# Attention and two mixtures of experts in one program: ScalarE, not SyncE, asks for the expert weights and for the stores of their split halves, one step later each

## The chip, the cores and the metric

The kernel runs on one core of a Trainium2 chip. The metric is device time in microseconds (us) of one execution; lower is better. A profile of one execution stands beside the timed runs.

## What is computed

Inputs are float32 (the two weights of the first feed-forward block arrive as 64-bit numbers and are converted on the chip). Three blocks follow each other:

```python
# 1: attention with 32 memory slots per head (8 batches, 8 heads, 576 positions, 64 wide)
a = softmax(phi); k_m = a^T k; v_m = a^T v
attn = softmax(q k_m^T / 8) v_m          # -> x: 4608 tokens x 512
# 2: a feed-forward block ("first MoE" in the kernel's names), 512 -> 2048 -> 512
x = relu(x @ w_in)**2 @ w_out
# 3: a mixture of 8 experts, one per token, 512 -> 1024 -> 512
e = argmax(x @ w_gate); out = gate * (relu(x @ w1[e]) @ w2[e])
```

Sums have to come out in about float32 accuracy, so a factor x is held as two float16 numbers, hi = f16(s x) and lo = f16(s x - hi), and each product is three matmuls.

## The kernel before

**Stages.** Until about 100 us the weights of block 2 are loaded and converted and the first batch goes through attention. From then to about 850 us the main loop (L1144) runs over 192 iterations n: 12 blocks of 384 tokens by 16 slices of the 2048 hidden columns. An iteration does `g1` (L656: six matmuls of U by attnT into the PSUM tile h, then three ScalarE operations L676, L678, L679 that make r = relu(h), g = r squared as float16 and r squared in float32, then one VectorE operation L680 that makes the low half of g) and, three iterations late, `g2` (L693: nine matmuls L688 of g by wo into acc). There are two buffers of h and four of g. From about 850 us the experts' tiles follow (`tiles`, L1225).

**What runs beside the main loop.** The seven other batches of attention are generators that are moved on in the loop (L1164 to L1181). A routing generator per token block (`route`, L729) makes record tiles rec, has them transposed by DMA (L760, xTb<-rec, asked for by SP), and scatters rows to DRAM (tile scr). `weight_stream` (L592) prepares the experts' weights: 16 matrices (w1 and w2 of eight experts), each in four quarters of 512 KB. Its four stage buffers are wst[c] (in the profile: wstage). For matrix n it takes a maximum of every quarter (w1: VectorE, L185 called from L618) or its sum of squares (w2: ScalarE, L616), works out a scale, and then for each quarter c: ScalarE writes the hi half into a buffer o (two of them; L643), VectorE the lo half (L644), SP stores o to DRAM (L645: ws1 or ws2 <- o) and SP asks for the same quarter of matrix n+1 (L597 or L599, called from L650). The buffers o are named wo in the profile (wo16 in the order of instructions).

**What sets the order.** Every engine works off its own list in order, and a DMA is asked for by an instruction in the list of SP, ScalarE or GpSimd. A scheduler with a simulated timeline puts each engine's list together when the program is built. The loop moves the weight stream on by WSTEPS / (16 * 10 - 4) steps per iteration (L1187); a step ends at a `yield`, of which a matrix has seven. Each DMA signals its landing on one of eight semaphores (DMAHW0 to DMAHW7) taken in turn, and an instruction that asks for a DMA first waits until the earlier DMA on its semaphore has landed.

Of the kernel before, what the change touches and what calls it, by code (L numbers as in the profile page):

```python
# [23 lines left out]
P = 128  # L24
B, H, S, D, M = 8, 8, 576, 64, 32
DM, DFF, NT, E, F = 512, 2048, 4608, 8, 1024
# [11 lines left out]
R0 = 3.0  # L38
R1 = 1.0
R2 = 2.5  # L40
WSTEPS = 2 * E * 7
HP0 = 50
HP1 = 50
UB = 3
# [9 lines left out]
def e23(x):  # L54
    return float(x * (1 << 23))
# [3 lines left out]
def tile_attention__then__moe__then__moe2(  # L59
# [14 lines left out]
    V, A, G, T, SP = nc.vector, nc.scalar, nc.gpsimd, nc.tensor, nc.sync  # L74
# [102 lines left out]
    def pow2_of_squares(t, s, total):  # L177

        ti, si = t.bitcast(I32), s.bitcast(I32)
        V.tensor_scalar(ti, total.bitcast(I32), 24, None, ALU.logical_shift_right)  # L180
        V.tensor_scalar(si, ti, e23(-1), e23(204), ALU.mult, ALU.add)
        V.tensor_scalar(ti, ti, e23(1), e23(59), ALU.mult, ALU.add)

    def absmax(dst, src):
        V.tensor_reduce(dst, src, axis=AX.X, op=ALU.max, apply_absolute_value=True)  # L185
# [406 lines left out]
    def weight_stream():  # L592
        def load(n, c):
            e, which = divmod(n, 2)
            t = wst[c]
            if which == 0:
                SP.dma_start(t, w1[e, c * P:(c + 1) * P, :])  # L597
            else:
                SP.dma_start(  # L599
                    t.rearrange("p (a n) -> p a n", a=2),  # L600
                    w2[e, 2 * c * P:(2 * c + 2) * P, :].rearrange("(a p) n -> p a n", p=P),
                )

        wstage = pw[0].tile([P, 4, 2 * DM], F32, tag="ws", name="wstage", bufs=1)
        wst = [wstage[:, c] for c in range(4)]
        for c in range(4):
            load(0, c)
        yield
        for n in range(2 * E):
            e, which = divmod(n, 2)  # L610
            m = pw[0].tile([P, 6], F32, tag="wm", name=f"wm{n}", bufs=2)
            sums = which == 1
            for c in range(4):
                if sums:
                    jk = wo[:, NF].rearrange("p a d -> p (a d)").bitcast(BF16)
                    A.activation(jk, wst[c], AF.Square, accum_out=m[:, c:c + 1])  # L616
                else:
                    absmax(m[:, c:c + 1], wst[c])  # L618
                if c % 2 == 1:
                    yield  # L620
            V.tensor_reduce(m[:, 4:5], m[:, 0:4], axis=AX.X, op=ALU.add if sums else ALU.max)
            G.partition_all_reduce(m[:, 5:6], m[:, 4:5], P, RED.max)
            yield
            top = 1 if which == 0 else 9
            t = pw[0].tile([P, 1], F32, tag="wt", name=f"wt{n}", bufs=2)
            s = pw[0].tile([P, 1], F32, tag="wsc", name=f"wsc{n}", bufs=2)
            ti, si = t.bitcast(I32), s.bitcast(I32)
            if sums:
                pow2_of_squares(t, s, m[:, 5:6])
            else:  # L630
                V.tensor_scalar(ti, m[:, 5:6].bitcast(I32), 0x7F800000, None, ALU.bitwise_and)
                V.tensor_scalar(ti, ti, e23(40), None, ALU.max)
                V.tensor_scalar(si, ti, -1.0, e23(254 + top), ALU.mult, ALU.add)
            V.tensor_scalar(winv[:, which, e:e + 1], t, 2.0 ** -top, None, ALU.mult)
            for c in range(4):
                o = pw[0].tile([P, 2 * F], F16, tag="wo16", name=f"wo16_{n}_{c}", bufs=2)
                if which == 0:
                    hi, lo, src = o[:, 0:F], o[:, F:], wst[c]
                else:
                    ov = o.rearrange("p (a x n) -> p a x n", a=2, x=2)  # L640
                    hi, lo = ov[:, :, 0, :], ov[:, :, 1, :]
                    src = wst[c].rearrange("p (a n) -> p a n", a=2)
                A.activation(hi, src, AF.Copy, scale=s)  # L643
                V.scalar_tensor_tensor(lo, src, s, hi, ALU.mult, ALU.subtract)  # L644
                SP.dma_start(  # L645
                    (ws1 if which == 0 else ws2)[e, 4 * c:4 * c + 4].rearrange("j p n -> p j n"),
                    o.rearrange("p (j n) -> p j n", j=4),
                )
                if n + 1 < 2 * E:
                    load(n + 1, c)  # L650
                yield
# [492 lines left out]
    for n in range(n_total + LAG):  # L1144
# [8 lines left out]
        if n < NF:  # L1153
            w_out_split(n)
        elif n == NF:
            ctx_start.close()
            pw[0] = ctx.enter_context(tc.tile_pool(name="pw", bufs=1, reuse_waits="tile"))
            wgen = weight_stream()
# [26 lines left out]
        if wgen is not None:  # L1185

            at["weights"] += WSTEPS / (NF * (NB - 2) - 4)  # L1187
            while wgen is not None and at["weights"] >= 1:
# [121 lines left out]
```

## Time and profile before

| what | value |
|---|---|
| time, median of 3 runs | 1264.56 us (1263.05 to 1271.3) |
| the profiled execution | 1263.46 us, of which the span of the instructions is 1261.8 us |
| mean granted TensorE clock | 0.973 |
| DMA issues of the weight stream | 64 loads (wstage<-in_moe_w_dram) and 64 stores (ws<-wo) of 512 KB, all by SP |

The profile names instructions by engine (PE is TensorE's matmul, PEld its weight load, DVE is VectorE, ACT ScalarE, POOL GpSimd, SP SyncE), by line of the kernel and by tile (out<-in, buffer numbers left out). ACTq and SPq are the list side of an engine: DMA issues, register work, waits on semaphores. Idle time is put down to what ended it.

### The profile page before, as it was taken

To read this page: it belongs to the slowest core of one execution; us is meant where nothing else is said; L and a number is where in the kernel's file an instruction comes from. 1 tells how busy PE (TensorE), PEld (TensorE's weight loads), DVE (VectorE), ACT (ScalarE), POOL (GpSimd) and SP (SyncE) were. 2 spreads that over 40 slices of the span, in tenths; PEclk is the share of its full clock that TensorE was granted. 3 is DMA by queue.
4 is the path that set the end of the run, shared out by engine and by line. 5 is a ranking of instruction groups with operands and counts; after the bars stand their busy time and mean duration, and the time that the engine had idled before them with its cause. 6 is when DMAs were issued, how large, how long until landed. Compare 5 with 4: busy or idle time off the path is not lost.

```text
span 1261.8 us, 20352 instructions
## 1 busy us (share of the span) xinstructions
PE 1157.6 (92%) x7306; PEld 612.8 (49%) x7306; DVE 654.6 (52%) x1687; ACT 650.8 (52%) x1315; POOL 116.2 (9%) x169
## 2 busy tenths in 40 slices
PE   2658998998999998999999999997999999999995
PEld 1325465444566555466565565543444444444442
DVE  6998886987869867766656343343111111111110
ACT  4668877796877867766656565531111111111110
POOL 1000001001010110011010100004000000000000
PEclk9769999998999998999999999999999999999998
DMA  9938389677788779673131010479557957458465
GB/s 323 319 98 218 114 205 245 186 233 221 214 240 232 231 216 274 179 204 72 26 82 27 26 35 18 122 171 279 114 102 194 261 133 193 101 142 193 101 146 144
DMA packets 310920, 209.36 MB, mean 166 GB/s; under 512 B 209311, under 2 KB 289183, under 8 KB 310816
## 3 DMA queue, kind: packets, MB, share of 16 engines
q1 hardware_dynamic: 279408, 161.70, 51.0%
q10 hardware_dynamic: 24768, 25.17, 6.4%
q0 software_dynamic: 6640, 21.16, 4.6%
q8 instruction: 59, 0.97, 0.3%
q14 instruction: 45, 0.37, 0.1%
HBM read 234.53 MB, written 55.76 MB: 230 GB/s over the span
## 4 chain that ended last, share of the span: by engine, by line
PE 53%; DMA 17%; DVE 13%; issue 9%; ACT 4%; POOL 1%; SPq 1%; POOLq 0%; ACTq 0%; DVEq 0%
PE acc L688 16%; PE e L1021 13%; PE e L1048 12%; PE h L668 8%; DMA wstage<-in_moe_w_dram 6%; DVE wo L644 2%; DMA q<-in_q_dram 2%; DMA scr<-rec,sl 1%; DMA xTb<-rec 1%; DMA gT<-g 1%; PE u L578 1%; DMA ws<-wo 1%; ACT wo L643 1%; DVE g L680 1%; PE st L482 1%
## 5 line engine op out<-in xcount | busy, mean ns | idle before, releaser
L688 PE MATMUL acc<-wo,g 128*128 128x512 f16 x1728 | 417.5, 381 | 7.9 <-DVE g L680 5.9
L688 PEld LDWEIGHTS <-g 128*128 128x128 f16 x1728 | 166.5, 99 | 179.9 <-issue 10.1
L668 PE MATMUL h<-attnT,U 128*128 128x384 f16 (+1 forms) x1536 | 230.2, 287 | 5.4 <-ACT attnT L512 2.6
L1033 DVE SCALAR_TENSOR_TENSOR g<-e,g 128x512 f16<-128x512 f32 x78 | 50.3, 686 | 306.0 <-ACT g L1032 306.0
L668 PEld LDWEIGHTS <-U 128*128 128x128 f16 x1536 | 139.5, 98 | 89.1 <-issue 18.7
L680 DVE TENSOR_TENSOR g<-r,g 128x384 f16<-128x384 f32 x192 | 105.8, 553 | 90.8 <-ACT r L679 88.4
L1021 PEld LDWEIGHTS <-xT 128*128 128x128 f16 x936 | 91.4, 98 | 121.0 <-DMA xT<-scr 8.1
L1048 PEld LDWEIGHTS <-gT 128*128 128x128 f16 x936 | 91.2, 98 | 115.6 <-DMA gT<-g 4.8
L676 ACT ACTIVATE r<-h 128x384 f32<-128x384 f32 x192 | 92.7, 484 | 74.1 <-PE h L668 64.9
L1032 ACT ACTIVATE g<-e 128x512 f16<-128x512 f32 x78 | 42.3, 594 | 169.7 <-PE e L1021 159.7
L1021 PE MATMUL e<-w,xT 128*128 128x512 f16 x528 | 119.1, 383 | 6.7 <-DMA xT<-scr 4.8
L1048 PE MATMUL e<-w,gT 128*128 128x512 f16 x528 | 117.6, 379 | 4.2 <-DMA gT<-g 3.3
L1061 ACT ACTIVATE y<-e,fac 128x512 f32<-128x512 f32 x39 | 26.8, 687 | 175.5 <-PE e L1048 169.1
L678 ACT ACTIVATE g<-r 128x384 f16<-128x384 f32 x192 | 99.7, 521 | 10.3 <-PE acc L688 6.2
L679 ACT ACTIVATE r<-r 128x384 f32<-128x384 f32 x192 | 99.5, 520 | 3.6
L1021 PE MATMUL e<-wo,xT 128*128 128x512 f16 x408 | 91.0, 379 | 1.5 <-DVE g L1033 1.4
L1048 PE MATMUL e<-wo,gT 128*128 128x512 f16 x408 | 90.9, 379 | 0.2 <-DMA gT<-g 0.2
L644 DVE SCALAR_TENSOR_TENSOR wo<-wstage,wsc,wo 128x1024 f16<-128x1024 f32 x64 | 81.1, 1278 | 18.0 <-ACT wo L643 17.4
L643 ACT ACTIVATE wo<-wstage,wsc 128x1024 f16<-128x1024 f32 x64 | 71.8, 1145 | 29.1 <-DMA ws<-wo 14.4
L91 POOL DMA_INDIRECT out_dram<-y,rt x39 | 38.0, 974 | 351.0 <-ACT y L1061 144.5
L91 POOL DMA_INDIRECT scr<-rec,sl x36 | 38.2, 1061 | 274.7 <-ACT r L676 109.2
L185 DVE TENSOR_REDUCE wm<-wstage 128x1 f32<-128x1024 f32 x32 | 38.9, 1214 | 18.4 <-DMA wstage<-in_moe_w_dram 18.4
(258 smaller groups left out, 1143.3 us busy)
## 6 DMA issues: line engine op xcount, KB each, us to landing
w<-ws ACTq DMA_DIRECT2D x36, 2048.0 KB
wo<-ws ACTq DMA_DIRECT2D x34, 2048.0 KB
wstage<-in_moe_w_dram SPq DMA_DIRECT2D x64, 512.0 KB
ws<-wo SPq DMA_DIRECT2D x64, 512.0 KB
kv<-in_k_dram SPq DMA_DIRECT2D x16, 576.0 KB
kv<-in_v_dram SPq DMA_DIRECT2D x16, 576.0 KB
q<-in_q_dram SPq DMA_DIRECT2D x64, 144.0 KB
raw_ring<-in_moe_w_out_dram SPq DMA_DIRECT2D x12, 512.0 KB
```

What stands on the lines that cost most here:

```text
L91: i = G.indirect_dma_start(out=dst[:, :], out_offset=bass.IndirectOffsetOnAxis(ap=index, axis=0), in_=src, in_offset=None, bounds_check=bo ...
L643: A.activation(hi, src, AF.Copy, scale=s)
L644: V.scalar_tensor_tensor(lo, src, s, hi, ALU.mult, ALU.subtract)
L668: T.matmul(bank[:, off:off + w], u_t[b][:, g, uh, f * P:(f + 1) * P], attnT[b][:, g, ah, s0:s0 + w], start=(x == 0), stop=(x == len(seq) - 1),
L676: A.activation(r, bank[:, 0:BLK], AF.Relu, scale=2.0 ** -10)
L678: A.activation(g[:, 0], r, AF.Square)
L679: A.activation(r, r, AF.Square)
L680: V.tensor_tensor(g[:, 1], r, g[:, 0], op=ALU.subtract)
L688: T.matmul(a, g[:, gh, tt * P:(tt + 1) * P], wo[:, f, wh, :], start=(f == 0 and x == 0), stop=(f == NF - 1 and x == 2),)
L1021: T.matmul(bank[hf], x[:, 4 * xh + c, :].bitcast(F16), w[:, c, wh * F + hf * 512:wh * F + (hf + 1) * 512], start=(c == 0 and xh == 0 and w ...
L1033: V.scalar_tensor_tensor(g[:, 1, cs], bank, 0.0, g[:, 0, cs], ALU.max, ALU.subtract)
L1048: T.matmul(a, gT[:, 8 * gh + f, :], w[:, f // 2, o:o + DM], start=(f == 0 and x == 0), stop=(f == 7 and x == 2),)
```

## The change

All 128 DMA issues of the weight stream move from SP (`SP.dma_start`) to ScalarE (`A.dma_start`). A new `yield` stands between the split of a quarter and its store, so a matrix has eleven steps, and WSTEPS rises from 2 * 8 * 7 to 2 * 8 * 11 to match.

```diff
-WSTEPS = 2 * E * 7
+WSTEPS = 2 * E * 11
...
             if which == 0:
-                SP.dma_start(t, w1[e, c * P:(c + 1) * P, :])
+                A.dma_start(t, w1[e, c * P:(c + 1) * P, :])
             else:
-                SP.dma_start(
+                A.dma_start(
                     t.rearrange("p (a n) -> p a n", a=2),
                     w2[e, 2 * c * P:(2 * c + 2) * P, :].rearrange("(a p) n -> p a n", p=P),
                 )
...
                 A.activation(hi, src, AF.Copy, scale=s)
                 V.scalar_tensor_tensor(lo, src, s, hi, ALU.mult, ALU.subtract)
-                SP.dma_start(
+                yield
+                A.dma_start(
                     (ws1 if which == 0 else ws2)[e, 4 * c:4 * c + 4].rearrange("j p n -> p j n"),
                     o.rearrange("p (j n) -> p j n", j=4),
                 )
```

In the changed file every line from L645 on stands one lower (L645 is L646, L676 is L677). ScalarE's list before, at the ninth matrix (wo16_9_c is its quarter c) in iteration 68, where the records of a token block are made too:

```order
L676 ACTIVATE r68_4060<-h68_4047 128x384
L678 ACTIVATE g68_4062<-r68_4060 128x384
L643 ACTIVATE wo16_9_0_6111<-wstage_1628,wsc9_6106 128x2x512
L643 ACTIVATE wo16_9_1_6186<-wstage_1628,wsc9_6106 128x2x512
L741 ACTIVATE rec0_768<-x2f3_0_3966,sm3_3989 128x512
L679 ACTIVATE r68_4060<-r68_4060 128x384
L741 ACTIVATE rec1_769<-x2f3_1_3974,sm3_3989 128x512
L741 ACTIVATE rec2_770<-x2f3_2_3982,sm3_3989 128x512
L676 ACTIVATE r69_4090<-h69_4077 128x384
L678 ACTIVATE g69_4092<-r69_4090 128x384
```

ScalarE's list in the changed kernel at the same place, with the semaphores that each row waits for (DVE is VectorE's, Activation ScalarE's own, DMAHW and DMASW those of DMA landings):

```order
L643 ACTIVATE wo16_9_0_6014<-wstage_1579,wsc9_6009 128x2x512 [waits DMAHW5_49,DVE_49]
L643 ACTIVATE wo16_9_1_6064<-wstage_1579,wsc9_6009 128x2x512 [waits DMAHW1_49]
L742 ACTIVATE rec0_768<-x2f3_0_3971,sm3_3992 128x512 [waits DMASW6_49]
L742 ACTIVATE rec1_769<-x2f3_1_3979,sm3_3992 128x512 [waits DMASW7_49]
L742 ACTIVATE rec2_770<-x2f3_2_3987,sm3_3992 128x512 [waits DMASW0_49]
L646 DMA ws2_74<-wo16_9_0_6014 128x4x512 [waits DVE_49]
L597 DMA wstage_1579<-in_moe2_w1_dram 128x1024 [waits DMAHW3_49]
L646 DMA ws2_74<-wo16_9_1_6064 128x4x512 [waits DMAHW4_49,DVE_49]
L677 ACTIVATE r69_4092<-h69_4079 128x384 [waits PE_49]
L597 DMA wstage_1579<-in_moe2_w1_dram 128x1024 [waits DMAHW5_49]
L679 ACTIVATE g69_4094<-r69_4092 128x384 [waits Activation_49]
```

Two stores and two loads now stand in ScalarE's list, three of them in a row ahead of the relu of iteration 69; the stores wait for VectorE, and three of the four for the landing of an earlier DMA.

SP's list before, at the same place (xTb3 are the transposes of the records, q20 and q21 loads of attention):

```order
L645 DMA ws2_74<-wo16_9_0_6111 128x4x512
L597 DMA wstage_1628<-in_moe2_w1_dram 128x1024
L760 DMA_TRANSPOSE xTb3_0_4041<-rec0_768 128x8x128
L645 DMA ws2_74<-wo16_9_1_6186 128x4x512
L760 DMA_TRANSPOSE xTb3_1_4043<-rec1_769 128x8x128
L760 DMA_TRANSPOSE xTb3_2_4045<-rec2_770 128x8x128
L597 DMA wstage_1628<-in_moe2_w1_dram 128x1024
L354 DMA q20_3900<-in_q_dram 96x6x64 x2
L354 DMA q21_3938<-in_q_dram 96x6x64 x2
```

And in the changed kernel:

```order
L345 DMA kv0_97<-in_v_dram 96x4x384
L336 DMA e_t_96<-in_phi_dram 96x8x192
L761 DMA_TRANSPOSE xTb3_0_4043<-rec0_768 128x8x128
L761 DMA_TRANSPOSE xTb3_1_4045<-rec1_769 128x8x128
L761 DMA_TRANSPOSE xTb3_2_4047<-rec2_770 128x8x128
L354 DMA q20_3905<-in_q_dram 96x6x64 x2
L354 DMA q21_3941<-in_q_dram 96x6x64 x2
```

SP is left with the loads of attention and the transposes. The last quarter is split in iteration 110 before and in iteration 111 after, so the stream ends at the same place of the loop.

## Rows read from the trace of the kernel before

**Rows 1.** The page: busy us of each engine over the span, share, instructions.
```profile
PE 1157.6 (92%) x7306; PEld 612.8 (49%) x7306; DVE 654.6 (52%) x1687; ACT 650.8 (52%) x1315; POOL 116.2 (9%) x169
```
**Rows 2.** Busy time by stretch: from:to, its length, engines' busy us, granted clock, DMA share, GB/s.
```profile
100.00:560.00 460.00, 435.34 (x3244) 250.52 (x3245) 362.14 (x870) 360.12 (x724) 38.44 (x45) 0.99 0.76 214
560.00:850.00 290.00, 287.29 (x1969) 162.68 (x1968) 144.59 (x452) 165.47 (x361) 18.55 (x20) 1.00 0.28 68
...
305.00:312.20 7.20, 5.47 (x19) 2.75 (x20) 7.20 (x23) 4.21 (x10) 0.46 (x1) 0.53 0.56 209
476.00:483.00 7.00, 7.00 (x32) 4.75 (x32) 3.02 (x10) 4.05 (x11) 0.36 (x2) 0.52 1.11 312
```
**Rows 3.** Waits of PE from 100 to 560 us: total us, times, longest.
```profile
PE acc L688 <- DVE g L680: 5.9, 2, 3.6
PE rk L794 <- DVE oh L781: 4.2, 3, 2.6
...
PE lg L818 <- DMA xTb<-rec: 1.3, 1, 1.3
```
**Rows 4.** Waits of ScalarE in the same stretch.
```profile
ACT pt L494 <- DVE pt L491: 15.2, 8, 8.8
ACT wo L616 <- DMA wstage<-in_moe_w_dram: 15.0, 13, 2.8
ACT wo L643 <- DMA ws<-wo: 14.4, 19, 2.5
...
ACT r L676 <- PE h L668: 4.6, 6, 1.3
```
**Rows 5.** Waits of VectorE in the same stretch.
```profile
DVE wm L185 <- DMA wstage<-in_moe_w_dram: 18.4, 15, 3.0
DVE wo L644 <- ACT wo L643: 17.4, 21, 2.3
...
DVE ojmx L360 <- DMA e_t<-in_phi_dram: 3.1, 1, 3.1
```
**Rows 6.** Waits of SP's list in the same stretch.
```profile
SPq L645 <- DVE wo L644: 151.9, 26, 29.9
```
**Rows 7.** The stream's DMA issues by line: ns min/median/max, first and last start.
```profile
L645 SPq DMA_DIRECT2D ws<-wo x64: 377/400/4507, 122.7 to 549.8; - x64
...
L597 SPq DMA_DIRECT2D wstage<-in_moe_w_dram x32: 349/512/1452, 100.7 to 503.0; - x32
...
L599 SPq DMA_DIRECT2D wstage<-in_moe_w_dram x32: 378/555/2001, 123.1 to 530.9; - x32
```
**Rows 8.** ScalarE's groups from 100 to 560 us: busy us, mean ns, idle before.
```profile
L643 ACT ACTIVATE wo<-wstage,wsc 128x1024 f16<-128x1024 f32 x64 | 71.8, 1145 | 29.1 <-DMA ws<-wo 14.4 <-DVE wsc L633 6.1 <-DVE oh L781 5.2
L678 ACT ACTIVATE g<-r 128x384 f16<-128x384 f32 x112 | 58.1, 520 | 3.2 <-PE acc L688 1.4
```
**Rows 9.** Timeline (start, us, what): ScalarE in the experts' stage.
```profile
960.15 0.69 ACT L1061 ACTIVATE y<-e,fac 128x512 f32<-128x512 f32 x1 [4.31 <-PE e L1048]
...
960.50 0.41 ACTq L1004 DMA_DIRECT2D wo<-ws  x1
```
**Rows 10.** Timeline: two quarters are split and the second one's store follows.
```profile
266.93 2.21 ACT L643 ACTIVATE wo<-wstage,wsc 128x1024 f16<-128x1024 f32 x2
268.13 2.48 DVE L644 SCALAR_TENSOR_TENSOR wo<-wstage,wsc,wo 128x1024 f16<-128x1024 f32 x2 [0.28 <-ACT wo L643]
...
271.42 0.41 SPq L645 DMA_DIRECT2D ws<-wo  x1
```
**Rows 11.** Timeline of SP at the place of the order shown above.
```profile
380.79 0.51 SPq L597 DMA_DIRECT2D wstage<-in_moe_w_dram  x1
382.33 3.49 SPq L760 DMA_TRANSPOSE xTb<-rec  x1
385.86 0.57 SPq L645 DMA_DIRECT2D ws<-wo  x1
386.54 4.76 SPq L760 DMA_TRANSPOSE xTb<-rec  x2
391.35 0.57 SPq L597 DMA_DIRECT2D wstage<-in_moe_w_dram  x1
```
**Rows 12.** A piece of the chain that ended last: start, us, a load until its landing.
```profile
269.87 5.28 DMA wstage<-in_moe_w_dram
```

## The prediction

> **What bounds the kernel now.** I read the page's busy shares first: TensorE is busy for 92% of the span and no other engine for more than 52% [rows 1]. Such shares mix stages, so I cut the span next. From 560 to 850 us TensorE is busy for 287.29 of 290 us; there only its own work counts. From 100 to 560 us, the stretch in which the weight stream runs (its first store starts at 122.7 and its last at 549.8 us [rows 7]), it is busy for 435.34 of 460 us, VectorE for 362.14 and ScalarE for 360.12 [rows 2]. What the change can win or lose lies here: TensorE's idle 460 - 435.34 = 24.7 us, and two stretches with a granted clock of 0.53 and 0.52, mostly the lower of the two levels, 1.2 GHz [rows 2]. They cost 7.2 x 0.47 + 7.0 x 0.48 = 6.8 us; the first comes behind a stretch in which TensorE stood for up to 3.6 us for g [rows 2, 3]. Together 31.5 us.
>
> The waits say who is behind. ScalarE is idle for 460 - 360.12 = 99.9 us, but only 4.6 us of that are for h, which TensorE makes; the larger ones are for VectorE's part of a softmax (15.2), for landings of stage loads (15.0) and for stores out of the two buffers o (14.4) [rows 4]. So ScalarE hardly ever waits for TensorE: it runs behind, and TensorE lives on its lead of three iterations. VectorE is alike: 18.4 us for stage loads and 17.4 us for ScalarE's hi half [rows 5]. The 151.9 us for which SP's stores wait for lo [rows 6] are no loss in themselves: SP is then early.
>
> For a rate of exchange I take this stretch itself: 99.9 - 4.6 = 95.3 us of ScalarE's standstill go with 31.5 us lost on TensorE, so about a third of each us that ScalarE stands arrives at TensorE; the rest is taken up by its lead. It is an estimate, made with waits that the scheduler had planned around.
>
> **What the change removes.** SP loses 128 issues. By the medians these are 64 x 0.400 + 32 x 0.512 + 32 x 0.555 = 25.6 + 16.4 + 17.8 = 59.8 us of its list [rows 7], and the waits for lo. Who waited for SP? Where the order is shown, the load of the second quarter stands behind three transposes, and SP gets to it at 391.35 us, 10.6 us after the first one [rows 11]. On ScalarE it no longer stands behind them. In all, what hangs on SP's requests is 15.0 + 14.4 us on ScalarE, 18.4 + 3.1 us on VectorE and 1.3 us on TensorE, 52.2 us [rows 3 to 5]. Most of it stays, since a load takes some 5.28 us to land whoever asks [rows 12], and requests will go out later than before (below). Bounds: nothing, or all of it. I take a quarter, 12 us: row 11's case is rare beside the 26 waits in which SP stood ready for lo and asked at once [rows 6].
>
> The Trainium skill, page "DMA: Bandwidth & Descriptors", section "Issuing engines are not separate DMA queues", says that DMAs started by different engines run on the same 16 DMA engines, and that spreading them saves only the sequencer's time for asking. By that rule the 12 us would be nothing and the sum below 4 us higher; no run here shows two such queues side by side in this stage.
>
> **What it adds to ScalarE's list.** First the asking itself. The only DMAs that ScalarE asks for before show that its list runs on under a running operation: the y operation runs from 960.15 to 960.84 us, and a request of 0.41 us starts at 960.50 [rows 9]. A single request behind an operation of 0.52 us [rows 8] thus costs nothing if it is a store (0.40) and about 0.08 us if it is a load (0.53 and the step to it). In the new order 71 of the 128 stand alone, 36 of them loads: 3 us. The other 57 stand in 19 pairs, five threes and one four; a pair takes 0.40 + 0.53 + 0.08 - 0.52 = 0.5 us, a three 0.95, a four 1.4: 9.5 + 4.8 + 1.4 = 15.7 us. Sum 18 us. Bounds: 0, and 59.8 us if nothing is hidden.
>
> Second, a store now holds ScalarE's list until lo is there, and queued behind it are the next relu and squares, for which L680 and then the nine matmuls L688 wait. The second of two lo ends 270.61 - 269.14 = 1.47 us behind its hi [rows 10], which is three operations of 0.52 us [rows 8]. The new order puts 58 of the 64 stores three or more operations behind their hi, and six only one or two: 6 x 1 us. Where VectorE is itself late the others wait too; I take as much again: 13 us. Bounds: 0, and 64 x 1.47 = 94 us.
>
> Third, the semaphores in turn. In the list of the changed kernel 53 of ScalarE's requests wait for a landing of something that SP asked for, 24 of these for a request that stands at most three iterations earlier. An iteration is 460 / 112 = 4.1 us here [rows 8] and a landing 5.28 us [rows 12]; the ten at one or two iterations' distance can be late, by 1 us each: 10 us. Bounds: 0, and 24 x 5.28 = 127 us.
>
> Requests also come later in time: before, the store started 0.81 us after lo (270.61 to 271.42 [rows 10]); now it waits for its place, which stands behind up to nine operations. That lengthens the stream's loop, but the stream ends in the same iteration by the order, and nothing reads the stored weights until after 850 us.
>
> **The sum.** 18 + 13 + 10 - 12 = 29 us more standstill of ScalarE; a third of it is 9.7 us, so 9.5 on the profiled execution's 1263.46 us: 1273.0 us. That execution stands 1.1 us below the median of the runs, 1264.56, inside their spread; I leave the forecast at 1273.0. If the cover of the issues were gone, the term of 18 would be 59.8 and the sum 14 us higher. Before 100 and after 560 us nothing is touched. By the skill's rule above it would be 1277.
>
> **The rivals.**
> - *SP's relief decides.* Everything that hangs on SP's requests goes (52.2 us), and the new issues stay hidden: 52.2 / 3 = 17.4 us less, 1246 us. For it: the transposes block 9 us of SP at one place [rows 11], and ScalarE and VectorE both wait some 15 to 18 us for landings. Against: those waits are short (at most 3.0 us each [rows 4, 5]), as a landing that is simply awaited.
> - *Nothing comes through.* ScalarE's 99.9 idle us swallow the 41, or relief and cost cancel: 1263.5 us. For it: each wait that ScalarE has now takes up lateness. Against: it waits for h for 4.6 us only.
> - *ScalarE becomes the bound, slower.* Its list does not run on under an operation in this dense stage, so issues cost 59.8 us, and stores wait twice what I take (26): 59.8 + 26 + 10 = 96 of its 99.9 idle us, a third 32 us, 1295 us. It decides from the point at which ScalarE's idle time in this stretch falls under some 40 us. For it: 360 busy us of 460 leave little. Against: rows 9.
> - *Landings on the other list, slower.* ScalarE stands for SP's loads: 24 waits of 2 us instead of 10 us in all, 38 us more, a third 13 us: 1286 us. For it: the two lists share eight semaphores and SP can be late. Against: the stream's 128 requests alone come every 427.1 / 128 = 3.3 us [rows 7], so even with as many others between them eight requests span 13 us, and a landing takes 5.28.
>
> **How the numbers follow.** No change is what a measurement cannot tell from it, about 1%, 12.6 us: 1252 to 1277. Chances: forecast 0.39 (its own range 1262 to 1283; 0.28 of it within 1%, 0.11 slower), relief 0.16 (0.13 faster, 0.03 within), nothing 0.13 (within), ScalarE bound 0.20 (0.19 slower, 0.01 within), landings 0.12 (0.10 slower, 0.02 within). So faster 0.13, same 0.47, slower 0.40. The range runs from 1252 to 1297: it holds the bulk of every case but the relief, whose centre lies below it.
>
> **What would show it.** Right: in the new profile ScalarE's list shows issues of 0.4 to 0.55 us mostly under running operations; in its waits L646 stands with VectorE's L644 for some 13 us and DMAs with landings for some 10; from 100 to 570 us TensorE's idle time is 30 to 38 us; after that nothing differs. Wrong: TensorE's idle time there falls under 20 us (relief), or ScalarE's waits for stores and landings exceed 50 us (the two slower rivals), or the time moves in another stage altogether.

## The result and the profile after

The changed kernel took 1284.59 us in the median of 3 runs (1275.6 to 1285.38) against 1264.56 us before: a ratio of 1.0103, with a 95% interval from 1.0062 to 1.0144. (The two medians alone lie 1.6% apart; with three runs each, spread over 8 to 10 us, they say less than the ratio.) Twelve later runs gave 1.0099 (1.0068 to 1.0130), a median of 1284.54 us beside 1271.69 us for 29 runs of the kernel before, which spread from 1264.49 to 1279.63 us. So the change costs about 1%, 12 to 13 us. The profiled execution of the changed kernel, 1284.59 us, is 21.1 us above the one before; about a third of that is chance, as the second profiles below show.

The page's busy shares of the changed kernel answer to [rows 1], and its DMA queues (packets, MB, share of 16 engines' span) show that the requests did move: before, q1 carried 161.70 MB and q10, ScalarE's, 25.17.

```profile
PE 1171.1 (91%) x7306; PEld 616.9 (48%) x7306; DVE 657.0 (51%) x1687; ACT 651.7 (51%) x1315; POOL 118.7 (9%) x169
...
q1 hardware_dynamic: 232304, 94.58, 34.2%
q10 hardware_dynamic: 71872, 92.28, 22.8%
```

Busy time by stretch (the columns of [rows 2]), and two of its short stretches at half clock:

```profile
100.00:560.00 460.00, 429.10 (x3121) 243.93 (x3119) 358.29 (x848) 353.06 (x708) 38.28 (x42) 0.97 0.74 207
560.00:850.00 290.00, 285.22 (x2006) 164.22 (x2007) 145.98 (x454) 171.28 (x369) 20.68 (x22) 1.00 0.30 75
...
284.20:291.00 6.80, 4.99 (x14) 1.90 (x15) 6.13 (x13) 6.01 (x15) 0.00 (x0) 0.50 0.80 236
325.20:332.00 6.80, 4.95 (x29) 4.57 (x30) 5.93 (x13) 6.00 (x12) 1.25 (x2) 0.50 0.87 206
```

In the weight stream's stretch TensorE is idle for 460 - 429.10 = 30.9 us (24.7 before), and the records of the granted clock have 27.3 us of it at 0.5 (13.7 before), of which half is lost: 44.5 us against 31.5, 13 us more. (TensorE also idles inside the half-clock time, as in the first row above, where it is busy for 4.99 of 6.80 us; so some 2 us are counted twice, 0.7 before.) The waits there, for PE, ScalarE, VectorE and SP's list, answer to [rows 3 to 6]:

```profile
PE h L669 <- ACT r L677: 5.1, 3, 3.7
PE lg L819 <- DMA xTb<-rec: 4.9, 1, 4.9
PE qTp L461 <- ACT qT L466: 4.9, 2, 2.6
PE acc L689 <- ACT g L679: 4.4, 2, 4.0
PE aT L508 <- ACT g L679: 4.3, 1, 4.3
...
PE acc L689 <- DVE g L681: 0.7, 1, 0.7
```

```profile
ACT wo L643 <- DMA ws<-wo: 25.0, 13, 5.0
...
ACT wo L616 <- DMA wstage<-in_moe_w_dram: 9.5, 7, 4.5
...
ACT pt L494 <- DVE pt L491: 2.8, 4, 1.0
```

```profile
DVE wm L185 <- DMA wstage<-in_moe_w_dram: 17.4, 12, 3.4
...
DVE ojmx L360 <- DMA e_t<-in_phi_dram: 13.4, 4, 6.5
```

```profile
SPq L761 <- DVE rec L743: 89.8, 3, 43.0
...
SPq L345 <- DMA ws<-wo: 47.3, 3, 22.4
```

Read them by who is waited for. Before, TensorE's longest waits were for VectorE; now they stand mostly against what ScalarE makes (r, qT, g), with 5.1 + 4.9 + 4.4 + 4.3 us; what ScalarE itself had waited for is followed back below. ScalarE in turn waits longer for stores to land (25.0 us, from 14.4), and less for VectorE's softmax part (2.8, from 15.2): it is later, so that part is ready. Five places in ScalarE's timeline (start, us, what, idle before) show how it comes to be late:

```profile
188.48 0.39 ACTq L646 DMA_DIRECT2D ws<-wo  x1
188.91 0.74 ACTq L599 DMA_DIRECT2D wstage<-in_moe_w_dram  x1
190.13 0.39 ACTq L646 DMA_DIRECT2D ws<-wo  x1
190.57 0.49 ACT L677 ACTIVATE r<-h 128x384 f32<-128x384 f32 x1 [2.16 <-DVE st L490]
190.59 1.33 ACTq L599 DMA_DIRECT2D wstage<-in_moe_w_dram  x1
191.97 0.52 ACT L494 ACTIVATE pt<-pt 96x384 f32<-96x384 f32 x1 [0.91 <-DVE pt L491]
...
197.46 1.15 ACT L643 ACTIVATE wo<-wstage,wsc 128x1024 f16<-128x1024 f32 x1 [2.80 <-DMA ws<-wo]
...
284.40 1.15 ACT L643 ACTIVATE wo<-wstage,wsc 128x1024 f16<-128x1024 f32 x1 [4.96 <-DMA ws<-wo]
284.40 0.39 ACTq L646 DMA_DIRECT2D ws<-wo  x1
285.45 0.51 ACT L679 ACTIVATE g<-r 128x384 f16<-128x384 f32 x1
...
403.56 0.52 ACT L679 ACTIVATE g<-r 128x384 f16<-128x384 f32 x1
407.56 0.35 ACTq L597 DMA_DIRECT2D wstage<-in_moe_w_dram  x1
408.00 0.21 ACT L769 ACTIVATE lg<-lg 128x48 f32<-128x48 f32 x1 [3.92 <-PE lg L821]
...
457.53 1.25 ACT L584 ACTIVATE U<-u,vts 128x512 f16<-128x512 f32 x2
461.51 0.39 ACTq L646 DMA_DIRECT2D ws<-wo  x1
461.94 0.49 ACT L677 ACTIVATE r<-h 128x384 f32<-128x384 f32 x1 [3.16 <-DVE wo L644]
```

From 188.48 four requests follow each other, of 0.39, 0.74, 0.39 and 1.33 us, and the relu and the pt operation have 2.16 and 0.91 us of idle time ahead of them. At 197.46 and 284.40 the hi operation has waited 2.80 and 4.96 us for a store to land, with qT and g behind it in the list. At 407.56 a load's request comes 3.5 us behind the end of the last operation (403.56 + 0.52): its semaphore had been taken by one of SP's transposes, which landed at 407.53 by the semaphore's record. At 461.51 a store's request has waited 2.73 us in the open for lo (458.78 to 461.51), which VectorE made late: a stage load had kept it waiting for 3.38 us. What the stores that landed late did to TensorE: it stood for that qT and that g, and the half-clock stretch from 284.20 above begins in the second stop. These are its stops of over 2 us between 105 and 560 us, seven in all:

```profile
198.96 0.74 PE L461 MATMUL qTp<-ident,q 96*128 96x96 f32 x3 [2.65 <-ACT qT L466]
280.60 1.46 PE L689 MATMUL acc<-wo,g 128*128 128x512 f16 x6
286.01 1.03 PE L689 MATMUL acc<-wo,g 128*128 128x512 f16 x2 [3.95 <-ACT g L679]
...
327.05 0.55 PE L508 MATMUL aT<-ident,pt 96*128 96x96 f32 x2 [4.29 <-ACT g L679]
377.69 0.38 PE L689 MATMUL acc<-wo,g 128*128 128x512 f16 x1 [2.97 <-ACT x2f L727]
396.97 1.22 PE L461 MATMUL qTp<-ident,q 96*128 96x96 f32 x6 [2.27 <-ACT qT L466]
407.58 0.28 PE L819 MATMUL lg<-wg,xTb 128*128 128x16 f16 x4 [4.95 <-DMA xTb<-rec]
484.41 1.14 PE L669 MATMUL h<-attnT,U 128*128 128x384 f16 x6 [3.69 <-ACT r L677]
```

They make 24.8 of its 30.9 idle us. Before the change there were three, of 2.6, 2.3 and 3.6 us, all for what VectorE makes. Each of the seven can be followed back to something that waited for a DMA to land. Before the stops at 198.96, 286.01, 396.97 and 484.41 (12.6 us) ScalarE's hi had waited 2.7 to 5.0 us for the landing of a store, and what TensorE needed stood behind that hi. Before 377.69 it was L616, which waited 4.46 us for a stage load; before 407.58 the transposes themselves. Before 327.05 it was VectorE, which waited for phi, with the low half of g behind that wait, and ScalarE's relu waited for this g:

```profile
324.20 0.69 DVE L360 TENSOR_TENSOR ojmx<-e_t 96x512 f32<-96x512 f32 x1 [6.54 <-DMA e_t<-in_phi_dram]
```

SP had asked for this phi at 311.74 us; before, it asked at 294.77. Phi takes as long to land as before (10.8 and 10.9 us in the mean), but SP's list, which the scheduler orders anew, comes to it later: loads of q ahead of it started at 294.68 us (before at 282.39), and a transpose, which now stands ahead of it too, at 308.29. The second profile has six of the seven stops, with the same waits ahead of them; the one at 396.97 is missing. So none of the long stops is ended by a request that ScalarE's list stood for directly; such standing uses up its lead, by this reading, and a landing on top of it then stops TensorE.

### The profile page after: what moved, and what is told of

Read it like the earlier page. It is cut to its first block, busy times and chain, and to the rows that moved or that the text cites. A ratio compares the mean times of both kernels' runs of the same rounds, so it can differ in the third digit from the quotient of the medians.

```text
span 1282.7 us, 20307 instructions
## 1 busy us (share of the span) xinstructions
PE 1171.1 (91%) x7306; PEld 616.9 (48%) x7306; DVE 657.0 (51%) x1687; ACT 651.7 (51%) x1315; POOL 118.7 (9%) x169
## 5 line engine op out<-in xcount | busy, mean ns | idle before, releaser
L669 PEld LDWEIGHTS <-U 128*128 128x128 f16 x1536 | 141.0, 99 | 96.9 <-issue 26.3
L677 ACT ACTIVATE r<-h 128x384 f32<-128x384 f32 x192 | 92.4, 484 | 89.4 <-PE h L669 70.9
L1022 PE MATMUL e<-w,xT 128*128 128x512 f16 x528 | 122.0, 389 | 10.4 <-DMA xT<-scr 10.0
L644 DVE SCALAR_TENSOR_TENSOR wo<-wstage,wsc,wo 128x1024 f16<-128x1024 f32 x64 | 81.4, 1281 | 15.4 <-ACT wo L643 15.2
L185 DVE TENSOR_REDUCE wm<-wstage 128x1 f32<-128x1024 f32 x32 | 38.8, 1213 | 17.5 <-DMA wstage<-in_moe_w_dram 17.4
```

What stands on the lines that cost most here:

```text
L669: T.matmul(bank[:, off:off + w], u_t[b][:, g, uh, f * P:(f + 1) * P], attnT[b][:, g, ah, s0:s0 + w], start=(x == 0), stop=(x == len(seq) - 1),
L677: A.activation(r, bank[:, 0:BLK], AF.Relu, scale=2.0 ** -10)
L1022: T.matmul(bank[hf], x[:, 4 * xh + c, :].bitcast(F16), w[:, c, wh * F + hf * 512:wh * F + (hf + 1) * 512], start=(c == 0 and xh == 0 and w ...
```

## The experiments

Of each kernel the table gives what its profile and records show beside its ratio. "Stage" is the time from the first relu r to the last (192 of them). "Asking" is ScalarE's idle time, from its first relu to its 113th, in gaps that hold one of its requests: the part before the request's row, the row itself, the rest. "Store" and "transpose" are means from the start of the request's row to the last completion signal on its semaphore, for requests from 100 to 560 us. "hi" is the wait of the hi operation for landings of ws in the stretch from 100 to 560 us.

| kernel | ratio (95%) | stage us | asking us | store us | transpose us | hi us |
|---|---|---|---|---|---|---|
| before, first profile | 1 | 725.1 | - | 5.12 | 4.60 | 14.4 |
| before, again | 1.0011 (0.9995 to 1.0028) | 727.2 | - | 5.11 | 4.58 | 12.2 |
| changed, first profile | 1.0103 (1.0062 to 1.0144) | 739.1 | 8.0 + 21.1 + 3.4 | 5.63 | 7.75 | 25.0 |
| changed, again | 1.0099 (1.0068 to 1.0130) | 733.0 | 7.6 + 18.1 + 3.5 | 5.54 | 7.40 | 21.9 |
| fine steps, SP asks | 1.0013 (0.9989 to 1.0037) | 733.7 | - | 4.89 | 4.66 | 13.0 |
| coarse steps, ScalarE asks | 1.0151 (1.0107 to 1.0194) | 750.9 | 5.3 + 24.0 + 6.2 | 5.41 | 5.31 | 16.1 |
| GpSimd asks | 1.0072 (1.0040 to 1.0104) | 746.5 | - | 5.42 | 5.40 | 16.0 |
| stores alone on ScalarE | 1.0134 (1.0103 to 1.0165) | 749.7 | 5.8 + 6.4 + 11.5 | 6.32 | 5.47 | 24.0 |
| loads alone on ScalarE | 1.0161 (1.0133 to 1.0189) | 748.6 | 5.4 + 8.1 + 4.2 | 6.77 | 4.81 | 40.7 |
| load ahead of store, SP | 1.0076 (1.0051 to 1.0101) | 733.8 | - | 6.43 | 5.61 | 19.9 |
| small copies on ScalarE | 1.0080 (1.0056 to 1.0103) | 736.6 | 17.6 + 19.1 + 20.1 | 4.96 | 4.27 | 1.9 |
| split, SP asks | 0.9971 (0.9953 to 0.9990) | 725.2 | - | 4.64 | 4.99 | 8.3 |
| split, fine, SP asks | 0.9964 (0.9939 to 0.9989) | 724.4 | - | 4.75 | 5.06 | 6.8 |
| split, fine, ScalarE asks | 1.0040 (1.0016 to 1.0065) | 738.6 | 13.7 + 20.7 + 13.7 | 4.64 | 5.92 | 4.0 |

A stage comes from one execution and differs by up to 6 us between two of the same kernel, so verdicts go by the ratios. So do comparisons with expected times: these were set on 1264.56 us, and the kernel before took 1266.85 to 1273.76 us in the median beside the later runs.

**Both kernels once more.**

> The changed kernel once more, profiled, to see what repeats. Between the two first profiles the weight stream's stage cost 14.2 us and the experts' stage behind 850 us another 7. If the experts' stage has really changed (its stored weights are the same and its list is the same), 1280 to 1286 us and the 7 us are there again; if that part is chance, 1273 to 1281 us in the median, with the stage behind 850 us within 3 us of before and the 10 to 14 us between 350 and 470 us again.

> The kernel before once more, profiled, since the runs of it spread from 1264 to 1280 us on this chip and the first profile (1263.46 us) stands below all of these. Asking, store waits and landings alike: TensorE loses more in the stretch from 100 to 560 us than the 31.5 us of the first profile when the execution is a typical one, some 35 to 40 us, with no single new wait; the difference between the two kernels is then about 10 us and not 21.

The stage behind the stream is chance. From the first y operation to the last it took 400.3 us in the first profile of before and 407.3 in the first of the changed kernel, but 408.0 in the second of before and 402.0 in the second of the changed one. The weight stream's stage kept its loss, 725.1 and 727.2 us against 739.1 and 733.0. The median, 1284.54, is where the first text put it for a real change behind 850 us, and yet both kernels show that stage at some 400 and at some 408 us. The second profile of the changed kernel is of its fastest run of twelve (1274.12 us), so it shows less than the usual loss. Of two executions near their medians, 1284.59 after and 1273.54 before (its second), the stream's stages differ by 739.1 - 727.2 = 11.9 us and the whole by 11.1: there the loss lies before 850 us. The expected 35 to 40 us on TensorE in a typical execution of before were not seen: 24.8 us idle (435.18 us busy in 460) and half of 10.2 us, 30 us. Only its stage behind 850 us was slower.

**The finer steps alone, and the engine alone.** From the changed kernel, its three requests were given back to SP; then, in another kernel, the step was taken out and ScalarE kept the requests.

```
 WSTEPS = 2 * E * 11          (fine, SP asks: kept)
                 yield        (kept)
-                A.dma_start(
+                SP.dma_start(
```

> SP asks for everything as before; only the finer steps stay (a step between the lo half and the store, 11 steps per half weight instead of 7). List (the loss comes from ScalarE's own list, which stands behind the asking, behind VectorE's lo and behind landings): 1261 to 1268 us, since ScalarE asks for nothing. Landings (requests of two lists take eight semaphores in turn, so that a load of SP waits for the landing of a store that ScalarE asked for late): 1261 to 1268 us too, since one list asks for all in the order of the program. Steps (the later place of stores and loads lengthens the stream's loop and starves both engines of buffers): 1275 to 1285 us, the whole loss, with over 20 us of ScalarE waiting for the stores' landings (L643).

```
-WSTEPS = 2 * E * 11
+WSTEPS = 2 * E * 7
...
-                yield
                 A.dma_start(
```

> ScalarE asks, but without the added step and with the old 7 steps per half weight. List: each store stands directly behind its hi and so waits for lo, about 1.47 us each, 64 x 1.47 = 94 us on ScalarE's list; at a third of it the loss grows to some 30 us, 1290 to 1300 us, and the wait of the store's line for VectorE reaches 60 us or more. Landings: as the changed kernel or a little better, 1272 to 1285 us, since the requests go out earlier. Steps: 1262 to 1268 us.

The steps cost nothing that the runs can tell, 1.0013, against 1.0099 for the changed kernel in as many runs: they are not the cause. This rests on the runs alone, for the stage in this kernel's one profile, 733.7 us, is as long as in the second one of the changed kernel. The coarse variant is slower than the changed kernel (1290.79 against 1284.54 us in the median, though the intervals overlap), as the list theory said, but not by its reason: ScalarE did not stand 60 us for lo. The time before requests is 5.3 us: in this trace three or more operations of ScalarE start between hi and store for 48 of the 64 stores, so the expected 94 us of waits had no ground. What makes it slower than the fine one was not found. TensorE's longest waits in it, from 100 to 560 us, are these:

```profile
PE acc L688 <- ACT x2f L726: 7.8, 1, 7.8
PE lg L818 <- DMA xTb<-rec: 7.0, 1, 7.0
```

**GpSimd asks.** The changed kernel with G.dma_start in the three places.

> The changed kernel with GpSimd asking in ScalarE's place; nothing of the stream's requests stands on ScalarE's or SP's list. List: the loss goes, 1258 to 1267 us, and ScalarE's idle time from 100 to 560 us falls back to 100 us or less. Landings: SP still shares the eight semaphores with another engine that asks late, so SP's loads still wait for landings of stores by some 50 us or more, and the time stays at 1273 to 1285 us. Steps: 1275 to 1285 us.

It is no free list. The requests go out on q0, a queue of another kind, and SP no longer waits for landings of ws; but GpSimd stands for lo itself, and its reductions (of the experts' maxima and of mx) are queued behind. The queue's row, and GpSimd's longest wait from 100 to 560 us:

```profile
q0 software_dynamic: 25072, 88.28, 20.3%
```

```profile
POOL ws L646 <- DVE wo L644: 126.1, 36, 6.7
```

The list theory's 1258 to 1267 us was missed, though ScalarE asks for nothing here. The 1.0072 may have causes of its own, so the run neither bears that theory out nor excludes it.

**One half of the requests on each list.**

```
stores:  A.dma_start((ws1 if which == 0 else ws2)...)   loads: SP.dma_start
```

> ScalarE asks for the stores alone, with the finer steps; SP asks for the loads. In this order 60 of the 64 requests stand alone on ScalarE's list and only two pairs are left. Asking (ScalarE's list stands while it issues two or three requests in a row; 18 to 21 us of its idle time in the two traces of the changed kernel): that term falls to a few us, so the loss falls to a third or less, 1.000 to 1.004 of before. Store waits (ScalarE held until VectorE's lo is there): the loss stays as with the full change, 1.006 to 1.012. Landings (SP's loads wait for a semaphore that a store asked for on the other list frees): it stays too, 1.006 to 1.012, and SP waits for landings of ws for some 70 us as it did with the full change.

```
loads:  A.dma_start(t, w1...), A.dma_start(t..., w2...)   stores: SP.dma_start
```

> ScalarE asks for the loads alone, each one alone on its list (60 single requests by the order); SP asks for the stores. Asking: a single request hides under a running operation, so 1.000 to 1.004 of before. Store waits: ScalarE is never held for lo, 1.000 to 1.003. Landings: ScalarE's loads share the semaphores with SP's stores, which come late; ScalarE stands for landings of ws in the loads' line, 1.004 to 1.012.

All six forecasts were too low: 1.0134 and 1.0161. The second is slower than moving all, clear of the intervals; for the first they overlap. Standing at requests was small (the rows took 6.4 and 8.1 us), so asking cannot be all of it. SP's list shows no wait for a landing of ws in either, so the landings theory fails in the form it had. What grew is the time from a store's request to its landing, 5.1 to 6.3 and 6.8 us, and with it hi's wait. With everything on one list a store goes ahead of the load of its step; here the two are on two lists, and each is asked for 0.03 us (median) behind lo, so that they start together. That they hold each other up is argued, not shown. The row of the second kernel:

```profile
ACT wo L643 <- DMA ws<-wo: 40.7, 17, 6.1
```

**The order on one list.** To test that without ScalarE, the kernel before was given one change:

```
+                if n + 1 < 2 * E:
+                    load(n + 1, c)
                 SP.dma_start((ws1 if which == 0 else ws2)...)
-                if n + 1 < 2 * E:
-                    load(n + 1, c)
```

> The kernel before, SP asking for everything, with one thing turned round: the load of the next stage buffer is asked for ahead of the store of the same step. ScalarE asks for nothing. Turn (on one list the store goes out alone, ahead of the load, and lands early, so that its o buffer is free in time; with two lists the two share the DMA engines, or other loads go beside the store, and it lands later): the mean time from a store's request to its landing grows from 5.1 us to 6.5 us or more, ScalarE's waits for o buffers (its hi line for landings of ws) from 12 to 14 us to 25 us or more, and the ratio is 1.006 to 1.015. Asking and store waits on ScalarE's list: neither occurs here, 0.998 to 1.003.

The store lands 1.3 us later, and the kernel loses 0.8% with no request on ScalarE. Hi waits 19.9 us, less than expected; but it waits 32.0 us for loads (15.0 before), though these land sooner (5.68 us against 6.30); why was not followed up. The scheduler's order of SP's other requests moved with the swap, which this run does not separate:

```profile
ACT wo L616 <- DMA wstage<-in_moe_w_dram: 32.0, 18, 4.4
ACT wo L643 <- DMA ws<-wo: 19.9, 16, 3.2
```

**Requests without transfers.** Fine steps, SP asks, and besides:

```
                 yield
+                A.dma_start(tiny[:, (8 * n + 2 * c + 0) % 8], o[0:1, 2 * F - 8:2 * F])
+                A.dma_start(tiny[:, (8 * n + 2 * c + 1) % 8], o[0:1, 2 * F - 8:2 * F])
                 SP.dma_start(
```

> The finer steps with SP asking for loads and stores (1.001 of before), and besides ScalarE asks twice in each of the 64 steps for a copy of 16 bytes out of lo, after the added step: 128 requests on its list that wait for lo and take the semaphores in turn, but move nothing. 104 stand alone, 12 pairs. The copies are extra work whose result is not used. Asking, store waits and semaphores on ScalarE's list: its list stands as in the changed kernel, 1.006 to 1.012. Turn: the large transfers keep their order on one list, 0.999 to 1.004, with the store's request to landing near 5 us.

The kernel pays 0.8% although the large transfers land as before (4.96 us). But the probe is not pure: a small copy takes 4.47 us to land, and hi then waits for it, because the copy reads o; so the loss is not that of the list alone:

```profile
ACT wo L644 <- DMA tiny<-wo: 20.0, 13, 4.2
```

**Hi and lo in buffers and stores of their own.** First with SP asking, on the kernel before; then with the finer steps, by either engine.

```
-                o = pw[0].tile([P, 2 * F], F16, tag="wo16", name=f"wo16_{n}_{c}", bufs=2)
+                oh = pw[0].tile([P, F], F16, tag="wo16h", name=f"wo16h_{n}_{c}", bufs=2)
+                ol = pw[0].tile([P, F], F16, tag="wo16l", name=f"wo16l_{n}_{c}", bufs=2)
...
                 A.activation(hi, src, AF.Copy, scale=s)
+                SP.dma_start(dh.rearrange("j p n -> p j n"), oh.rearrange("p (j n) -> p j n", j=2))
                 V.scalar_tensor_tensor(lo, src, s, hi, ALU.mult, ALU.subtract)
-                SP.dma_start(
...
+                SP.dma_start(dl.rearrange("j p n -> p j n"), ol.rearrange("p (j n) -> p j n", j=2))
```

> The kernel before with hi and lo in buffers and stores of their own (256 KB each): hi goes out before lo is made, and its buffer is free earlier. SP asks for 64 stores more. Turn (what counts is how early the store that ScalarE waits for lands): ScalarE's waits for landings of ws fall from 12 to 14 us to under 6 us, and the ratio is 0.993 to 0.999. Asking and store waits on ScalarE's list: 0.998 to 1.003, for nothing is asked for by ScalarE; SP's 64 requests more are beside its path.

> Hi and lo in buffers and stores of their own, SP asks, with the finer steps (the added step ahead of the lo store): the same as the split without them, 0.994 to 1.001, as the finer steps alone were worth 1.001. Turn: hi's waits for landings of ws stay near 8 us. Asking: ScalarE asks for nothing, 0.994 to 1.003.

> The changed kernel with hi and lo in buffers and stores of their own: ScalarE asks for 192 transfers instead of 128, and the store for which its next hi waits goes out earlier. Turn (the changed kernel loses because its stores land later, beside SP's transfers): the waits of hi for landings of ws fall from 22 to 26 us to under 12 us, and most of the loss goes, 0.998 to 1.005. Asking (it loses because ScalarE's list stands while it asks and waits): 64 more requests, 100 of the 192 alone, 39 groups of two to four; the standing behind requests grows from 30 us to 40 us or more, and the ratio is 1.010 to 1.016 in spite of earlier stores. If both hold, the two nearly cancel: 1.005 to 1.010.

With SP the split is faster than the kernel before, twice, by 0.3 to 0.4%; hi waits for stores 8.3 and 6.8 us. With ScalarE asking, the stores land just as early (4.64 us) and hi's wait is down to 4.0 us, and the kernel is still slower:

```profile
ACT wo16h L647 <- DMA ws<-wo16h: 4.0, 4, 1.5
```

Between the two last kernels only the asking engine differs, and what the scheduler makes of it: 1.0040 over 0.9964 is 0.8%, and the intervals do not meet. For the unsplit pair it is 1.0099 over 1.0013, 0.9%. So the loss comes with ScalarE's asking and not with the finer steps, and in the split kernel not with late stores either.

For the changed kernel that last point stays open. By its expectation the split was to give back most of the loss if late stores were the cause (0.998 to 1.005), and none if standing at requests was (1.010 to 1.016): 1.0040 met the first and missed the second. It is true that the split gains about as much with SP asking (1.0013 to 0.9964, against 1.0099 to 1.0040). But with ScalarE it adds 64 requests, and the time in gaps with requests grows from 29 and 33 us to 48 (13.7 + 20.7 + 13.7), which may have taken back what the earlier stores gave.

## Why the prediction was right, and where its steps were not

1273.0 us meant 9.5 us more; the ratios say 12.5 to 13, so the direction was right and the size near, and 1284.59 lies in the whole range, though above the forecast's own (1262 to 1283). The mechanism was right in part: ScalarE's list does stand for what it asks for, by some 30 us, but TensorE's long stops come behind landings, most of them of stores, and the sum had counted waits for landings as a gain. TensorE's idle time from 100 to 570 us, forecast at 30 to 38 us, is 32.0 in the first profile and 29.2 in the second, against 24.9 before. "Nothing differs after 560 us" holds to 2 or 3 us: from the 113th relu to the last it took 270.0 and 270.4 us before, 272.6 and 272.2 after. The profile's other 7 us are chance.

- *The issue itself, 18 us.* Rows in the open took 18.1 and 21.1 us; some 84 of the 128 requests ran wholly under operations. This term was right. (Its parts add up to 18.7; this and the other roundings, 12 as 13 and 9.7 as 9.5, change nothing.)
- *Stores waiting for lo, 13 us, and landings on the other list, 10 us.* Both were too large. By the semaphores' records ScalarE stood idle 4.1 us for lo in either profile, 2.7 and 2.5 of it at the one store shown at 461.51. For landings of what SP had asked for it stood 3.5 and 3.1 us, most of it at the transpose shown at 407.56, and 0.7 us for one of its own loads. With the rows and the steps to them that makes 33 and 29 us of the 41.
- *"Now it waits for its place".* This failed. A store's request starts 0.03 us (median) behind lo in both kernels, and in the mean 0.15 to 0.20 us behind it, against 0.44 before. The requests go out earlier.
- *Relief, 12 us.* This failed in sign. The waits that were to shrink came to 52.2 us; the same five are 9.5 + 25.0 + 17.4 + 13.4 + 4.9 = 70.2 us (64.6 in the second profile). Only those for stage loads fell. The median store lands as before (5.08 us), but 13 and 11 of the stores took over 8 us, against 7 and 8 before and 4 with the finer steps alone. The stores for which hi waited at 197.46 and 284.40 landed 9.0 and 10.0 us after their requests (188.48 and 274.39), which followed SP's loads of attention within 3 us; that these held them up was not tested. Phi comes late by SP's new order. SP's transposes land in 7.4 to 7.75 us instead of 4.60, but in 5.31 with coarse steps, where ScalarE asks as well; why was not found.
- *A third of each us.* This failed as a rate. Over the same 112 iterations ScalarE's idle time grows from 96.9 to 108.2 us and the time itself from 455.1 to 466.4: with the same work, the one is the other. Of these 11.3 us TensorE idles 5.5 more, and as many are lost to its half clock (27.3 us at 0.5 instead of 13.7). Of the new standing, some 30 us, part was swallowed where ScalarE used to wait (pt, 15.2 to 2.8). That a wrong sum times a wrong rate came near is luck in part.
- *The rivals.* Relief is excluded, since the waits grew; so is 1295, since most requests are hidden and ScalarE is still idle for 106.9 of the 460 us. The landings rival's 1286 is nearer to 1284.59 than 1273.0 is, but its 48 us of ScalarE standing for SP's requests were 3.5. SP's 47.3 us for landings of ws hang on little: its next buffer was mostly still being read when the landing came (one landed at 259.77, the request went out at 273.26). What is shown is that ScalarE's asking costs 0.8 to 0.9%; how its list's standing, the stores that land late and SP's new order share that was not separated.

The Trainium skill, "DMA: Bandwidth & Descriptors", section "Issuing engines are not separate DMA queues", says that requests of different engines interleave on the same 16 DMA engines and save the sequencer's time only. The runs agree that nothing was won; that 1277 by that rule is what the ratio gives (1264.56 x 1.0103 = 1277.6) is no proof of it, since the other terms of that sum were off. The runs add a price: a store landed in 6.3 to 6.8 us where its load was on another list, and ahead of it on the same one in 4.9 to 5.1 us on SP's and in 5.4 to 5.6 us on ScalarE's.

## What to carry to other kernels

An engine that does nothing but ask may stand for long without loss, as SP did here; before moving its requests to an engine with work, look for the waits that really hang on it, and expect them to stay or grow. One list also keeps an order: the store that frees a buffer ahead of the load, and requests that are split over two lists can lose it. The requests that stay behind get a new order too, and one that slips, like phi here, can stop the engine that matters. To find out what a change costs, follow the long stops of the bounding engine back to what ended them, before adding up the idle time of another. If a buffer's release is what is late, store its first half as soon as it is made (here 0.3 to 0.4% faster than the kernel before, SP asking).

## What the runs showed that was not expected

- The same two transfers, asked for by SP in the other order, cost 0.8%: the store took 6.43 us to land instead of 5.12. (SP's other requests moved with it.)
- A copy of 16 bytes took 4.47 us to land among the large ones, hardly less than a store of 512 KB in the same kernel (4.96).
- Moving half of the requests cost 1.3 and 1.6%, moving all 1.0%; only for the loads alone is that clear of the intervals.
- The same kernel's stage behind 850 us took 400.3 or 408.0 us, so a single pair of profiles can be 7 us off.
